# A landmark attention and two feed-forward layers in one kernel: the attention's pool released earlier, its last batch planned with more lead, two unit orders changed

## The chip, the cores and the metric

One core of a Trainium2 chip runs the whole program in one launch. The metric is the device time of that core in microseconds (us). The engines are TensorE (PE in the profile, its weight loads PEld), VectorE (DVE), ScalarE (ACT) and GpSimd (POOL); SyncE (SP) issues all DMAs of this kernel from one in-order queue. [...]

## The reference, cut to what matters

Shapes: `q`, `k`, `v` are 4 batches x 8 heads x 576 x 64; there are 2304 tokens of width 512; the first layer is 512 to 2048 to 512, the second 512 to 1536 (gate and value) to 512.

```python
A, Bm, C = sm(q, k_lm), sm(q_lm, k_lm), sm(q_lm, k)      # 32 landmarks: means over 18 rows
Z = Bm.T / (norm1(Bm) * norminf(Bm) + 1e-06)
for _ in range(6):
    Z = 2 * Z - Z @ Bm @ Z
x = A @ Z @ C @ v                                         # attention, then (B*S, H*D)
h = x @ w_in
x = np.maximum(0.01 * h, h) @ w_out                       # first layer
xn = x / np.sqrt(np.mean(x * x, -1, keepdims=True) + 1e-06) * rms_g
g, val = xn @ w_gate, xn @ w_val
out = (g * (1.0 / (1.0 + np.exp(-g))) * val) @ w_out2     # second layer
```

## The kernel before

Products are made in float32 precision out of three TensorE products of rounded parts: each operand is split into a `hi` and a `lo` (copy with rounding, then subtraction), and hi*hi, lo*hi, hi*lo are summed in PSUM. The splits keep VectorE, ScalarE and GpSimd busy beside TensorE.

Tokens go in blocks of 288: batch b is blocks j = 2b and 2b+1, eight in all. Three stages follow one another on TensorE.

**Attention and first layer.** For each batch and head group g, `chain` makes the Newton iteration and the small tile `wt` out of q, k and v; `form_m` multiplies `wt` with `w_in` into the weights `mm` of that batch (four column parts c, four buffers); `soft_a` makes the left softmax `at` of a block. The k buffers are two, so the k of batch 3 is loaded (`load_k`) when `soft_a` of block 5 has read those of batch 2. A unit (j, f) of the first layer is `ffn1_h` (L768) and `ffn1_y` (L834); there are 128, and the last ones are blocks 6 and 7. A finished block's sum goes to DRAM (L861), later `norm(j)` loads it (L982), squares it (L994 to L1000), lets TensorE sum over the features (L1005), and scales it (L1041); `load_x` (L1062) brings the two blocks of a batch back and `prep_x(b)` makes the seven split right-hand sides X of batch b (a Strassen-like scheme of seven products).

**Gate and value.** A unit (f, b) of the second layer, `gv`, has seven products of six matmuls (L1116), with seven additions and products after them on VectorE (`gv_rest`, L1171 to L1207), then a store of the result (L1198). `prep_w(f)` splits the weights W(f) into one of two homes, "even" and "odd", so W(f) can be made only when W(f-2) is through. The order of the 48 units is the list `seq`, written out by hand.

**Output.** `load_o` (L1256) loads the seven prepared tiles of `w_out2` (1536 KB each) into the homes that X and W leave: B11 and T2 where X(0) was, T3 and T1 where X(1) was, B21 and T4 where the last two W were, B22 where X(3) was. `load_u` (L1291) loads the results, `prep_u` splits them, and `out_pair` (L1359) makes nine pairs of 128-row blocks with seven products each.

Where things lie decides what can start: `att` is the pool of the attention; when it is released, `open_p2a` allocates the second layer's pool (`p2a`: loads of y, scratch, W "even", X(0)) in its place, and an instruction waits in hardware only for those old tiles that lie under its own. X(1) takes the space of the first half of `w_out` (free when no unit uses it any more), X(2) that of the second half (free after the last unit of the first layer), X(3) that of `mm` and `at`.

The order of every engine's instructions is fixed beforehand by a planner (`Order`). Each piece of work is a generator that yields an engine with an estimated duration and the conditions for it. The planner keeps its own clock and takes, among the pieces that can start soonest, the one with the smallest due time; a due time is a place in the list of units minus a lead from `PAR`. `pause(n)` is a wait of n ns that it assumes, for a DMA for instance. On the chip each engine then follows its list in order, and waits where the estimate was too short. `("cc", 1)` asks for one of the two buffers of a ring.

Of the kernel before, what the change touches and what calls it, by code (L numbers as in the profile page):

```python
# [8 lines left out]
F32 = mybir.dt.float32  # L9
F32R = mybir.dt.float32r  # L10
U32 = mybir.dt.uint32
# [7 lines left out]
P = 128  # L19
M = 32  # L20
# [5 lines left out]
PAR = {  # L26
    "bias": {"dve": 0, "act": 0, "pool": -300},
    "window": 100,
    "slope": 16.25,
    "t0": 25300,  # L30
    "unit": 2400,
    "chain": [18400, 20600, 27900, 42200],
    "soft": 5000,
    "form": 2600,
    "conv": 600,
# [4 lines left out]
    "h": 700,  # L40
    "y": -3900,
    "norm": 90000,
    "last": 60000,
    "second": 36800,
    "unit2": 5600,
    "pair": 14900,
# [133 lines left out]
def dvep(n):  # L180
    return [("dvep", int(n * 1.04) + 67)]
# [18 lines left out]
def pause(ns=0):  # L200
    return [(None, ns)]
# [3 lines left out]
def landmark_attention_then_two_ffns(  # L205
# [14 lines left out]
    B, NP, _, S = qT.shape  # L220
    NG = NP // 2
# [30 lines left out]
    def new(tag, pool, shape, dtype=F32):  # L252
        t = pool.tile(shape, dtype, tag=tag, bufs=rings[tag], name=tag)
        order.taken(tag, t)
        return t
# [38 lines left out]

    p1 = tc.alloc_tile_pool(name="p1", bufs=1, side="left", reuse_waits="tile")
    conv = tc.alloc_tile_pool(name="conv", bufs=1, side="right", reuse_waits="tile")
    att = tc.alloc_tile_pool(name="att", bufs=1, side="right", reuse_waits="tile")

    w_in_sb = [att.tile([P, NP, 512], U32, name=f"w_in{c}") for c in range(NC)]
    NFA = 8  # L300
    wo_hi, wo_lo = {}, {}
    home = {}
# [179 lines left out]
    def chain(b, g):  # L482
# [166 lines left out]
                order.free(pr)  # L649
        yield pe4(64), [(pa, 2), ("wt", 1), f"cv{b},{g}"]  # L650
        pw = bank(pa), bank(pa)
        wt = new("wt", att, [P, 2, M])
        for h, p, rows, lm in heads():
            nc.tensor.matmul(
                pw[p][rows, :M], t1[lm, :], z[lm, :], start=True, stop=True
# [219 lines left out]
    def open_p2a():  # L875
        pool = tc.alloc_tile_pool(name="p2a", bufs=1, side="right", reuse_waits="tile")
        p2["a"] = pool
        p2["ones"] = pool.tile([P, P], F32, name="ones")
        nc.gpsimd.memset(p2["ones"], 1.0)
        p2["power"] = pool.tile([P, 3], F32, name="power")  # L880
        nc.gpsimd.memset(p2["power"], -0.5)
        for i in range(2):
            home[i] = pool.tile([P, 4096], F32R, name=f"q{i}")
        home["even"] = pool.tile([P, 7 * KD * P], F32R, name="wt")
        home["y"] = pool.tile([P, 3, KD * SB], F32, name="yin")
        home["misc"] = pool.tile([P, 4 * 2 * SB + 2 * KD * P], F32, name="misc")
# [17 lines left out]
    def new_y():  # L904
        return spot("y_in", 0, (KD, SB))


    opened = {0: "p2a", 1: "p2a", 2: "w1_free", 3: "w1_free", 4: "w2_free", 5: "w2_free",
              6: "m_all", 7: "m_all"}

    def quarter(i, shape, dtype=F32R):
# [64 lines left out]
    def norm(j):  # L976

        if j < NB - 1:
            before = [f"normed{j - 1}"] if j else []
            yield sp(P * 16 * SB), ["p2a", f"y{y_of[j]}", ("y_in", 1)] + before  # L980
            y = new_y()
            nc.sync.dma_start(y, y_dram[y_of[j]])  # L982
            order.done(f"normed{j}")
            yield pause(3000), []
        else:
            yield pause(0), [f"y{y_of[j]}"]
            y = y_in[j]
        e = yield act(SB) + dvep(SB), [("tt", 2)]
        ss = [new_tt() for _ in range(2)]
        for d in range(KD):  # L990
            if d:
                e = yield act(SB) + dvep(SB), []
            if e == "act":
                nc.scalar.activation(ss[d // 2][:, d % 2, :], y[:, d, :], AF.Square)  # L994
            else:
                nc.vector.tensor_mul(ss[d // 2][:, d % 2, :], y[:, d, :], y[:, d, :])
        e = yield pool_dve(2 * SB), []
        engine[e].tensor_add(ss[0], ss[0], ss[1])
        e = yield pool_dve(SB), []
        engine[e].tensor_add(ss[0][:, 0, :], ss[0][:, 0, :], ss[0][:, 1, :])  # L1000

        yield pe4(40, 3), [("pa", 1)]
        pn = bank("pa")
        for t in range(3):
            nc.tensor.matmul(  # L1005
                pn[:T96, SB + t:SB + t + 1], ss[0][:, 0, t * T96:(t + 1) * T96],
                p2["ones"][:, :1], start=True, stop=True,
            )
        rr = p2["a"].tile([T96, 4, 3], F32, tag="rr", bufs=2, name="rr")
        yield dve(3), []  # L1010
        nc.vector.tensor_scalar(
            rr[:, 0, :], pn[:T96, SB:SB + 3], 1.0 / DM, EPS_RMS, op0=ALU.mult, op1=ALU.add
        )
        order.free(*ss)
        yield [("pool", 1000)], []
        nc.gpsimd.tensor_tensor(rr[:, 1, :], rr[:, 0, :], p2["power"][:T96, :], op=ALU.pow)

        yield dvep(3), []
        nc.vector.tensor_mul(rr[:, 2, :], rr[:, 1, :], rr[:, 1, :])
        yield dvep(3), []  # L1020
        nc.vector.scalar_tensor_tensor(
            rr[:, 3, :], rr[:, 2, :], -0.5, rr[:, 0, :], op0=ALU.mult, op1=ALU.mult
        )
        yield dvep(3), []
        nc.vector.scalar_tensor_tensor(
            rr[:, 2, :], rr[:, 3, :], 1.5, rr[:, 1, :], op0=ALU.add, op1=ALU.mult
        )
        yield dvep(SB), []
        dg = p2["a"].tile([T96, 3, T96], F32, tag="dg", bufs=1, name="dg")
        nc.vector.tensor_tensor(  # L1030
            dg, ident[:T96, :T96].unsqueeze(1).to_broadcast([T96, 3, T96]),
            rr[:, 2, :].unsqueeze(2).to_broadcast([T96, 3, T96]), op=ALU.mult,
        )
        yield pe4(SB), []
        nc.tensor.matmul(
            pn[:, :SB], p2["ones"][:T96, :], dg.rearrange("p t n -> p (t n)"),
            start=True, stop=True,
        )
        for d in range(KD):
            yield dve(SB), []  # L1040
            nc.vector.scalar_tensor_tensor(  # L1041
                y[:, d, :], y[:, d, :], g_sb[:, d:d + 1], pn[:, :SB],
                op0=ALU.mult, op1=ALU.mult,
            )
        order.free(pn)
        if j == NB - 1:
            order.done(f"x{j}")
            return
        yield sp(P * 16 * SB), []
        nc.sync.dma_start(y_dram[y_of[j]], y)  # L1050
        yield pause(2500), []
        order.free(y)
        order.done(f"xn{j}")

    def load_x(b):
        js = [j for j in (2 * b, 2 * b + 1) if j < NB - 1]
        yield sp(P * 16 * SB * len(js)), [f"xn{j}" for j in js] + [("y_in", len(js))] + (
            [opened[2 * b], opened[2 * b + 1]] if b < B - 2 else [f"normed{NB - 2}"]
        ) + ([f"y_in{b - 1}"] if b else [])
        for j in js:  # L1060
            y_in[j] = new_y()
            nc.sync.dma_start(y_in[j], y_dram[y_of[j]])  # L1062
        order.done(f"y_in{b}")
        yield pause(3000), []
        for j in js:
            order.done(f"x{j}")

# [36 lines left out]
        order.free(y0, *(y_sum[len(segs) - 1] if b == B - 1 else [y1]), ta, tb)  # L1104


    seq = [(f, b) for f, b in zip((0, 1, 0, 1, 0, 0, 1, 1), (0, 0, 1, 1, 2, 3, 2, 3))]
    seq += [(f, b) for f in range(2, NF2 - 2) for b in range(B)]
    seq += [(f, b) for bs in ((0, 1), (2,), (3,)) for f in (NF2 - 2, NF2 - 1) for b in bs]
    place = {k: i for i, k in enumerate(seq)}  # L1110

    def product(pp, f, b, i, k, first):
# [318 lines left out]
    with tc.manual_schedule():  # L1431
        def due(u):

            return PAR["t0"] + PAR["unit"] * u
# [75 lines left out]

        def start_second():
            yield pause(0), [f"a{NB - 1},{g}" for g in range(NG)] + [
                f"m{B - 1},{c},{g}" for c in range(NC) for g in range(NG)
            ]
            att.release()
            open_p2a()
            order.done("p2a")
            for j in range(NB):
                order.add(due2(j // 2), PAR["norm"], norm(j))
            for b in range(B):  # L1520
                order.add(due2(place[0, b]), PAR["prep"], load_x(b))
                order.add(due2(place[0, b]), PAR["prep"], prep_x(b))
            for f in range(NF2):
                order.add(due2(place[f, 0]), PAR["prep"], prep_w(f))
            order.add(due2(0), 0, gv(0))
            for i, k in enumerate(o_order):
                order.add(due_o(0) + i * PAR["pair"] // 7, 2 * PAR["prep"], load_o(k))
            for n in range(NG2):
                order.add(due_o(n), PAR["load_u"][min(n // 2, 1)], load_u(n))
                order.add(due_o(n), PAR["prep_u"], prep_u(n))  # L1530
            order.add(due_o(0), 0, out_pair(0))

        order.add(due(len(units)), PAR["second"], start_second())
        order.run()
        p2["a"].release()
        state["p1b"].release()
        p1.release()
        conv.release()


# [50 lines left out]
```

## Time and profile before

| | us |
|---|---|
| median of 3 runs (862.51 to 866.36) | 866.31 |
| the profiled execution's own time | 863.65 |
| its span, first to last instruction | 861.6 |
| TensorE busy | 825.5 |
| VectorE busy | 626.3 |
| ScalarE busy | 342.6 |
| GpSimd busy | 151.1 |

The first two stages end at about 438.8 and 715.9 us of the span. Busy is the union of an engine's instructions; matmuls are pipelined and their ends are modelled. In the timeline a row is the start, the length, the engine, the line, the operation, the tiles written and read, and how many instructions are merged; what stands in brackets is the idle time ahead of it and what ended it.

### The profile page before, as it was taken

The numbers are of one execution on the slowest core, as the hardware profiler recorded it, in microseconds if no ns is written. First come the engines' busy times: TensorE is split into PE (matmuls) and PEld (weight loads), VectorE is DVE, ScalarE is ACT, GpSimd is POOL, SyncE is SP. The second block draws the span as 40 slices with busy tenths as digits, with TensorE's granted clock in tenths as the row PEclk, the third lists the DMA queues.
The fourth block names the chain that finished last, engine by engine and source line by source line (L and its number), as shares of the span: only waits on it lengthen the run. The fifth ranks groups of instructions, "written<-read, shape, count | busy, mean of one in ns | idle before, by whom it ended". The sixth has DMA issues, their size and how long they took to land. (4 is left out here: it accounts for less than half of the span.)

```text
span 861.6 us, 17827 instructions
## 1 busy us (share of the span) xinstructions
PE 825.5 (96%) x6902; PEld 758.9 (88%) x6902; DVE 626.3 (73%) x1403; ACT 342.6 (40%) x814; POOL 151.1 (18%) x187
## 2 busy tenths in 40 slices
PE   4799999999999999999987999999999998999998
PEld 1488789988788786999887999999999998999998
DVE  6699784556565843768689877777777669799892
ACT  3676464445334633644534343333332223122120
POOL 2242241002120620122011312211222101000000
PEclk9599999999999999999989999999999999999999
DMA  9874774453723700566431223322221199663611
GB/s 326 319 250 144 244 238 144 165 186 101 221 89 110 238 30 1 181 203 229 141 110 56 91 104 106 105 104 105 105 102 45 64 349 380 189 183 98 180 42 49
DMA packets 80549, 131.97 MB, mean 153 GB/s; under 512 B 6224, under 2 KB 50256, under 8 KB 79568
## 3 DMA queue, kind: packets, MB, share of 16 engines
q1 hardware_dynamic: 80464, 130.84, 45.6%
q8 instruction: 54, 0.88, 0.4%
q14 instruction: 31, 0.25, 0.1%
HBM read 87.95 MB, written 42.86 MB: 152 GB/s over the span
## 5 line engine op out<-in xcount | busy, mean ns | idle before, releaser
L834 PE MATMUL py<-g_hi,w 128*128 128x288 f32 x1024 | 212.3, 300 | 0.0
L834 PEld LDWEIGHTS py<-g_hi,w 128*128 128x128 f32 x1024 | 165.0, 190 | 13.0 <-issue 12.1
L834 PE MATMUL py<-g_lo,w 128*128 128x288 f32 x512 | 151.6, 296 | 0.0
L768 PE MATMUL ph<-at,mm 128*128 128x288 f32 x768 | 127.4, 305 | 0.6 <-ACT hs L787 0.4
L768 PEld LDWEIGHTS ph<-at,mm 128*128 128x128 f32 x768 | 109.4, 191 | 15.5 <-ACT hs L787 4.8
L784 ACT ACTIVATE g_hi<-ph 128x288 fp32r<-128x288 f32 x128 | 52.5, 410 | 122.4 <-PE ph L768 107.7
L834 PEld LDWEIGHTS py<-g_lo,w 128*128 128x128 f32 x512 | 97.1, 190 | 0.0
L790 DVE TENSOR_TENSOR g_lo<-hs,g_hi 128x288 fp32r<-128x288 f32 x100 | 47.0, 470 | 57.0 <-ACT hs L787 54.6
L787 ACT ACTIVATE hs<-ph 128x288 f32<-128x288 f32 x128 | 52.1, 407 | 0.0
L1210 ACT ACTIVATE cc<-cc 128x288 f32<-128x288 f32 x48 | 21.4, 445 | 74.3 <-DVE cc L1207 74.3
L1116 PE MATMUL py<-w,wt 128*128 128x288 f32 x288 | 43.7, 302 | 4.2 <-DVE g_lo L1174 4.2
L1181 ACT ACTIVATE hs<-ph 128x288 f32<-128x288 f32 x48 | 19.7, 410 | 64.5 <-PE ph L1116 64.4
L1116 PEld LDWEIGHTS py<-w,wt 128*128 128x128 f32 x288 | 41.0, 194 | 4.5 <-DVE g_lo L1174 4.4
L1116 PE MATMUL py<-w,mm 128*128 128x288 f32 x288 | 42.6, 296 | 0.2 <-DVE g_lo L1174 0.2
L368 ACT ACTIVATE raw<-raw 128x512 f32<-128x512 f32 x52 | 35.3, 681 | 16.9 <-DMA raw<-w_val 10.1
L1184 DVE TENSOR_TENSOR cc<-g_hi,py 128x288 f32<-128x288 f32 x48 | 21.6, 450 | 26.7 <-PE py L1116 26.0
L1116 PEld LDWEIGHTS py<-w,mm 128*128 128x128 f32 x288 | 39.6, 188 | 0.7 <-DVE g_lo L1174 0.4
L790 POOL TENSOR_TENSOR g_lo<-hs,g_hi 128x288 fp32r<-128x288 f32 x28 | 23.8, 849 | 84.8 <-ACT hs L787 84.0
L735 PE MATMUL pa<-w_in,wt 64*32 64x512 f32 x256 | 33.7, 626 | 2.3 <-DVE x L689 1.3
L330 ACT COPY hs<-ph 128x288 f32<-128x288 f32 (+1 forms) x45 | 17.2, 382 | 43.6 <-PE ph L1359 36.6
L330 ACT CAST w<-misc 128x768 fp32r<-128x768 f32 (+1 forms) x23 | 17.6, 779 | 38.8 <-DVE misc L1329 20.7
L745 DVE TENSOR_TENSOR mm<-pa,mm 128x512 fp32r<-128x512 f32 x32 | 22.0, 689 | 15.2 <-ACT mm L330 15.0
(300 smaller groups left out, 1755.4 us busy)
## 6 DMA issues: line engine op xcount, KB each, us to landing
u_dram<-us SPq DMA_DIRECT2D x48, 288.0 KB, 2.1
wo_dram<-ct SPq DMA_DIRECT2D x42, 256.0 KB, 2.3
raw<-w_out SPq DMA_DIRECT2D x20, 512.0 KB, 4.4
y_dram<-ys SPq DMA_DIRECT2D x60, 144.0 KB, 2.5
yin<-y_dram SPq DMA_DIRECT2D x14, 576.0 KB, 4.4
yin<-u_dram SPq DMA_DIRECT2D x20, 384.0 KB, 6.2
raw<-w_gate SPq DMA_DIRECT2D x12, 512.0 KB, 4.0
raw<-w_val SPq DMA_DIRECT2D x12, 512.0 KB, 4.7
```

The source lines that it names most:

```text
L330: nc.scalar.copy(out, src)
L368: nc.scalar.activation(high.bitcast(F32), high.bitcast(F32), AF.Prelu, scale=2.0 ** -112, alpha=2.0 ** 32)
L735: nc.tensor.matmul(pm[lm, :], wt_in[b, g][rows, p], w_in_sb[c][rows, 2 * g + p, :].bitcast(F32), start=True, stop=True,)
L745: nc.vector.tensor_sub(lo, pm, hi.bitcast(F32))
L768: nc.tensor.matmul(ph[:, :SB], w[b, c][:, g, o:o + P], x[j][:, g, :], start=(n == 0), stop=(n == 3 * NG - 1),)
L784: nc.scalar.activation(g_hi[u], ph[:, :SB], AF.Prelu, alpha=0.01)
L787: nc.scalar.activation(hs, ph[:, :SB], AF.Prelu, alpha=0.01)
L790: engine[e].tensor_sub(g_lo[u], hs, g_hi[u].bitcast(F32))
L834: nc.tensor.matmul(yacc[i][d][:, :SB], w[f][:, d * P:(d + 1) * P], x[u], start=(f == f0 and n == 0), stop=(f == f1 - 1 and n == 2),)
L1116: nc.tensor.matmul(pp[:, :SB], w[f][:, i, c * P:(c + 1) * P], x[b][1][:, k, c, :], start=(first and n == 0), stop=(n == 5), skip_group_che ...
L1184: nc.vector.tensor_add(f32("c21", "cc"), t["u2"], pp["c"][:, :SB])
L1210: nc.scalar.activation(t["c12"], t["c12"], AF.Silu)
```

## The change

Six things are changed.

1. `w_in` and `wt` move out of `att` into a pool of their own, `wq`; the homes of X(0) are now made in `wq`, where `w_in` was (`free_w_in`), when the last `form_m` is through. `att` is released when the last `chain` and the last `soft_a` are through, and no longer waits for `form_m`.
2. The due time of the chain of batch 3 (with the loads of its k, q and v) lies 75000 ns ahead of its first unit and no longer 42200; `soft_a` and `form_m` of batch 3 lie 75000 ahead and no longer 60000.
3. The planner assumes 4200 ns and no longer 3000 for the loads of `norm` and `load_x`.
4. The scratch tile `dg` of `norm` is taken from the ring `cc` of the second layer.
5. `seq` begins (0,0) (1,0) (0,1) (1,1) (0,2) (1,2) (0,3) (1,3); the third pair was (0,2) (0,3), the fourth (1,2) (1,3).
6. `seq` ends (10,0) (11,0) (10,1) (11,1) and so on; it was (10,0) (10,1) (11,0) (11,1), then as now.

```diff
-    "chain": [18400, 20600, 27900, 42200],
+    "chain": [18400, 20600, 27900, 75000],
-    "last": 60000,
+    "last": 75000,
...
-    w_in_sb = [att.tile([P, NP, 512], U32, name=f"w_in{c}") for c in range(NC)]
+    w_in_sb = []
+    for i in range(2):
+        t = wq.tile([P, 4096], U32, tag=f"q{i}", name=f"w_in{i}")
+        t = t.rearrange("p (c a n) -> p c a n", a=NP, n=512)
+        w_in_sb += [t[:, 0], t[:, 1]]
...
-        wt = new("wt", att, [P, 2, M])
+        wt = new("wt", wq, [P, 2, M])
...
-        for i in range(2):
-            home[i] = pool.tile([P, 4096], F32R, name=f"q{i}")
...
-    opened = {0: "p2a", 1: "p2a", 2: "w1_free", 3: "w1_free", 4: "w2_free", 5: "w2_free",
+    opened = {0: "w_in_free", 1: "w_in_free", 2: "w1_free", 3: "w1_free", 4: "w2_free", 5: "w2_free",
...
-            yield pause(3000), []
+            yield pause(4200), []
...
-        yield dvep(SB), []
-        dg = p2["a"].tile([T96, 3, T96], F32, tag="dg", bufs=1, name="dg")
+        yield dvep(SB), [("cc", 1)]
+        cc = new("cc", p2["a"], [P, SB])
+        dg = cc[:T96, :].rearrange("p (t n) -> p t n", n=T96)
...
+        order.free(cc)
...
-        yield pause(3000), []
+        yield pause(4200), []
...
-    seq = [(f, b) for f, b in zip((0, 1, 0, 1, 0, 0, 1, 1), (0, 0, 1, 1, 2, 3, 2, 3))]
+    seq = [(f, b) for f, b in zip((0, 1, 0, 1, 0, 1, 0, 1), (0, 0, 1, 1, 2, 2, 3, 3))]
-    seq += [(f, b) for bs in ((0, 1), (2,), (3,)) for f in (NF2 - 2, NF2 - 1) for b in bs]
+    seq += [(f, b) for bs in ((0,), (1,), (2,), (3,)) for f in (NF2 - 2, NF2 - 1) for b in bs]
...
-                f"m{B - 1},{c},{g}" for c in range(NC) for g in range(NG)
+                f"chain{B - 1},{g}" for g in range(NG)
...
+        def free_w_in():
+            yield pause(0), [f"m{B - 1},{c},{g}" for c in range(NC) for g in range(NG)]
+            for i in range(2):
+                home[i] = wq.tile([P, 4096], F32R, tag=f"q{i}", name=f"q{i}")
+            order.done("w_in_free")
+
+        order.add(due(len(units)), PAR["second"], free_w_in())
```

## Rows read from the trace of the kernel before

**Rows 1.** The page, part 1: busy time, share of the span, instructions.

```profile
PE 825.5 (96%) x6902; PEld 758.9 (88%) x6902; DVE 626.3 (73%) x1403; ACT 342.6 (40%) x814; POOL 151.1 (18%) x187
```

**Rows 2.** Who waited for whom: total us, times, longest; TensorE's, then SyncE's at 410 to 440.

```profile
PE pa L1005 <- DVE misc L1000: 4.4, 2, 3.8
PE py L1116 <- DVE g_lo L1174: 4.4, 2, 4.2
...
PE py L1359 <- DMA mm<-wo_dram: 2.1, 1, 2.1
...
SPq L982 <- DMA y_dram<-ys: 5.6, 1, 5.6
```

**Rows 3.** Stretches: length, busy (instructions) of each engine, granted clock, DMA share, GB/s.

```profile
428.90:432.70 3.80, 0.01 (x1) 0.01 (x1) 2.96 (x6) 1.74 (x6) 0.00 (x0) 0.77 0.04 13
432.70:437.50 4.80, 4.78 (x22) 4.80 (x23) 3.30 (x8) 1.23 (x2) 1.31 (x1) 0.50 0.00 0
438.80:475.40 36.60, 31.63 (x222) 30.52 (x221) 34.72 (x76) 14.58 (x28) 5.51 (x6) 0.95 0.25 93
...
475.40:715.90 240.50, 240.50 (x1808) 239.99 (x1807) 178.79 (x377) 80.34 (x181) 48.87 (x52) 1.00 0.36 122
715.90:738.70 22.80, 18.16 (x136) 17.64 (x135) 20.01 (x32) 3.58 (x6) 0.00 (x0) 0.93 1.04 366
```

**Rows 4.** Timeline of SyncE's queue, 415 to 425, then ScalarE at 428.

```profile
415.88 0.92 SPq L1062 DMA_DIRECT2D yin<-y_dram  x2
416.90 1.73 SPq L861 DMA_DIRECT2D y_dram<-ys  x3
424.42 0.32 SPq L982 DMA_DIRECT2D yin<-y_dram  x1
...
428.34 0.45 ACT L994 ACTIVATE misc<-yin 128x288 f32<-128x288 f32 x1 [2.38 <-DMA yin<-y_dram]
```

**Rows 5.** Timeline: batch 3's keys and last chain product, last `form_m`, second `norm` load.

```profile
279.95 0.83 SPq L441 DMA_DIRECT2D kt<-kT  x2
...
334.89 0.32 PE L654 MATMUL pa<-rz,t 32*64 32x32 f32 x8
...
343.32 1.92 PE L735 MATMUL pa<-w_in,wt 64*32 64x512 f32 x16
...
347.62 0.42 SPq L982 DMA_DIRECT2D yin<-y_dram  x1
```

**Rows 6.** Timeline of VectorE while TensorE waits at 468 to 472.

```profile
469.56 1.42 DVE L929 TENSOR_TENSOR at<-misc,mm 128x576 fp32r<-128x576 f32 x2
470.90 0.44 DVE L1171 TENSOR_TENSOR g_hi<-hs,pa 128x288 f32<-128x288 f32 x1
...
471.93 0.44 DVE L1174 TENSOR_TENSOR g_lo<-g_hi,py 128x288 f32<-128x288 f32 x1
```

**Rows 7.** Timeline: `prep_w(2)` on ScalarE, GpSimd and VectorE.

```profile
479.92 0.61 ACT L330 CAST wt<-misc 128x512 fp32r<-128x512 f32 x1
...
485.32 0.73 POOL L965 TENSOR_TENSOR misc<-misc 128x256 f32<-128x256 f32 x1
...
485.44 1.16 DVE L929 TENSOR_TENSOR wt<-misc,wt 128x512 fp32r<-128x512 f32 x1 [0.32 <-ACT wt L330]
...
487.79 0.69 DVE L929 TENSOR_TENSOR wt<-misc,wt 128x512 fp32r<-128x512 f32 x1
```

**Rows 8.** Timeline: DMA issues at the end of gate and value, then TensorE's output stage.

```profile
687.51 0.32 SPq L1256 DMA_DIRECT2D q<-wo_dram  x1
...
719.59 0.43 SPq L1256 DMA_DIRECT2D mm<-wo_dram  x1
...
734.08 3.63 PE L1359 MATMUL py<-mm,at 128*128 128x256 f32 x18 [2.09 <-DMA mm<-wo_dram]
...
742.09 4.43 PE L1359 MATMUL py<-w,w 128*128 128x256 f32 x36
...
757.08 4.43 PE L1359 MATMUL py<-w,w 128*128 128x256 f32 x36
```

More of the change, by code (lines that the diff above doesn't have):

```diff
@@ L296, in landmark_attention_then_two_ffns @@
     conv = tc.alloc_tile_pool(name="conv", bufs=1, side="right", reuse_waits="tile")
+    wq = tc.alloc_tile_pool(name="wq", bufs=1, side="right", reuse_waits="tile")
     att = tc.alloc_tile_pool(name="att", bufs=1, side="right", reuse_waits="tile")
-    w_in_sb = [att.tile([P, NP, 512], U32, name=f"w_in{c}") for c in range(NC)]
+    w_in_sb = []
[3 more added lines that the diff above has]
+        w_in_sb += [t[:, 0], t[:, 1]]
     NFA = 8
@@ L1035, in norm @@
         nc.tensor.matmul(
-            pn[:, :SB], p2["ones"][:T96, :], dg.rearrange("p t n -> p (t n)"),
-            start=True, stop=True,
+            pn[:, :SB], p2["ones"][:T96, :], cc[:T96, :], start=True, stop=True,
         )
+        order.free(cc)
         for d in range(KD):
@@ L1537, in landmark_attention_then_two_ffns @@
         p1.release()
+        wq.release()
         conv.release()
```

## The prediction

> **What bounds the kernel now.** I read the page's busy times first: TensorE is busy 96% of the span, so whatever helps has to remove TensorE waits, and there are only 36 us of them, start-up and end included [rows 1]. The list of waits comes second: outside the start-up two of the three longest, 3.8 and 4.2 us, are waits for VectorE, in L1005 (the sum of a norm) and L1116 (gate and value); the third is a wait of the output stage for a DMA [rows 2]. The table of stretches shows what stands around them [rows 3], and that the middle of gate and value, 475.4 to 715.9, has no idle time at all: nothing is to be had there.
>
> Place A, end of the first layer. TensorE is idle from 428.9 to 432.7 and then runs until 437.5 at a granted clock of 0.50, the lower of its two levels [rows 3]. That is 3.8 us and half of 4.8: 6.2 us. The cause is `norm(6)`: its load was issued at 424.4, because SyncE had waited 5.6 us for the store of the same block [rows 2], and that store had shared the DMA engines with `load_x(1)`, issued at 415.9 between its pieces [rows 4]. The squares then waited another 2.4 us for the data, and TensorE, in order, stood behind L1005.
>
> Place B, first units of gate and value. A unit takes 240.5 / 43 = 5.59 us in the undisturbed middle; the five units from 438.8 to 475.4 took 36.6 instead of 28.0, so 8.6 us are lost [rows 3]. VectorE is busy 34.7 of those 36.6 us. In the 4.2 us wait it split X(3) for the next unit, while the addition that TensorE wanted, L1171, stood behind [rows 6]. VectorE is the bound here.
>
> Place C, first pair of the output. A pair takes 757.1 - 742.1 = 15.0 us [rows 8]. Going back two products of 2.14 from 742.1, the second pair began at 737.8, and the first took 21.9 us from 715.9: 6.9 us lost, 4.6 of them idle, the rest at a lower granted clock [rows 3]. The DMA engines are full in this stretch (share 1.04), and the last tile, B22, issued at 719.6, let TensorE go on at 734.1 [rows 8].
>
> Together 21.7 us lie in A, B and C. No row shows a fourth place as large that the change could reach.
>
> **The change part by part.** The sums are against the profiled execution's own 863.65 us; the median of the runs shown is 2.7 above it.
>
> *Earlier chain, pool given back earlier.* The chain of batch 3 starts with loads at 280 and ends at 335; the last `form_m` runs at 343, and the second norm's load comes at 347.6 [rows 5]. The load of the keys waits for buffers that `soft_a` of block 5 frees, and that due time is unchanged, so the chain can't start much before 280. With 33 us more lead it ranks ahead of the first layer's units and should end some 15 us sooner (estimate: the 55 us from load to end contain room for that, since its Newton steps alternate with units). `att` then goes back at about 320, not 345, and norms 0 to 5 and the split of X(0) move into the first layer by some 25 us. X(1) needs `w_out`'s first half, whose last use is 16 units of 18 matmuls before the stage's end; at 5.59 / 42 = 0.133 us a matmul [rows 3] that is 38 us before 438.8, about 400. Its loads come then, some 15 us before the 415.9 of now.
>
> What that is worth at A: the store of block 6 no longer shares the queue with `load_x(1)`, so the 5.6 us wait of SyncE shrinks to a normal landing, by 3 to 4 us, and VectorE doesn't split X(1) in the same microseconds. The longer assumed latency puts L1005 another 1.2 us back in TensorE's list. 3.8 us of idle time are covered by 3.5 + 1.2, and without the idle time I expect no stretch at 0.50. Between 0 and 6.2, I take 5.2.
>
> *First order.* X(3) is wanted by the seventh unit and not the sixth: 33.5 us after the stage's start, not 28.0. VectorE's bill up to there: an instruction on 288 columns takes the queue for 0.36 us and one on 576 for 0.67 (1.34 for two; 1.03 for one of each) [rows 6]. A unit has seven or eight of the small ones, some on other engines: 2.7 us. So five units cost 13.5, and of 36.6 busy us some 22 were other work (the end of norm 6, norm 7, X(2), X(3)). Before, the bill was 13.5 + 22 = 35.5 against 28.0: 7.5 short, near the 8.6 measured. After, norm 6 ends before the stage (2 us less): 6 x 2.7 + 20 = 36.2 against 33.5: 2.7 short. The difference is 4.8. Bounds: 0, if other work moves in, and 8.6.
>
> The price stands in `prep_w(2)`. W(2) goes where W(0) is, and W(0) is through one unit later, so one unit and not two covers its preparation. That took from 479.9 to 488.5, 8.6 us [rows 7]. W(0)'s last product ended near 475.4 + 5.6 = 481.0, so the first cast began 1.1 us ahead of that; the last part is wanted by the third product of the next unit but one, 5.6 + 1.6 = 7.2 us after it. 8.6 - 1.1 - 7.2 leaves 0.3 us late: nearly covered, by nothing to spare. [...] A piece of W(2) took 1.16 us on VectorE while GpSimd worked on another, and 0.69 alone [rows 7]. [...]
>
> *Last order.* X(0) is through one unit, 5.6 us, earlier, so the loads of B11 and T2 go out at about 682 and not 687.5 [rows 8], and those of the results likewise. From 687.5 to 734 the DMA engines work off one backlog (share 1.04 at its end). If it starts 5.6 us earlier, B22 lands at 728.4; the seventh product wants it at 715.9 + 6 x 2.14 = 728.7. T4 and B22 still can't leave before the last unit ends: two of 1536 KB at 366 GB/s are 8.6 us, which fits. The splits of the results start earlier too, and with them goes the wait for VectorE in this pair. Between 0 and 6.9, I take 5.3. W(11) is squeezed as W(2) is, with VectorE less loaded.
>
> *The rest.* `dg` in the ring `cc` holds one of two buffers for one product of norm 7; a unit's addition may wait for it, less than 1 us. `w_in` in its own pool costs no instruction. For this, the two W and possible waits of a chain that runs closer to its producers I take 1.3 (0 to 4.4, the total that any VectorE wait of a norm or unit shows now [rows 2]).
>
> Sum: 5.2 + 4.8 + 5.3 - 1.3 = 14.0. 863.65 - 14.0 = 849.7 for an execution like the profiled one, 852.3 if it shifts with the median; I take 851.
>
> **The rivals.**
> *The pool isn't given back earlier in fact.* For it: the chain hangs on key buffers [rows 5], and the hardware already waits tile by tile, so the planner's place means less than it seems. Then A keeps all but 1.2 us, B gains only by its order (6 x 2.7 + 22 - 33.5 = 4.7 short, 2.8 better), C stays 5.3, less 1.3: 8.0, or 857.
> *The tail is bound by bandwidth and by SyncE's order.* For it: the loads of T3 and T1 stand behind the results' loads, and T4 and B22 are issued when the last unit ends in either order. Then C gives 0 to 1: 9.2 in all, or 855.5.
> *The waits only move.* A planner that reorders everything may open as much as it closes: 861 to 868, about 864.
> *Slower: the squeezed W.* VectorE is still behind when W(2) is to be made, right after X(3). If a preparation takes 13.5 us and not 8.6, it is 5.2 late; TensorE idles that long and then runs at 0.50 as after A (2.4): 7.6 for each W. Two of them take 15.2 and the 14 are gone; this is the point from which it decides. At twice 8.6 it is 8.9 late, 11.3 each, 22.6 in all: about 873 less what remains, 872. Against it: VectorE has 25% free from 475 on [rows 3], and W(11) comes in such a stretch.
>
> **How the numbers follow.** Forecast 0.57 (its own range 845 to 857, from A 4 to 6, B 2.5 to 7, C 3 to 6.5); pool 0.16; tail 0.13; waits move 0.07; squeezed W 0.07. A measurement of this kernel can't tell less than 0.5%, 4.3 us, from no change. All of the forecast and nearly all of the next two lie beyond it: faster 0.84; the rest of these and most of the moved waits: same 0.09; slower 0.07. The range runs from 844 (nearly all of A, B and C) to 860 (the worse half of the two small-gain rivals); it leaves out the last two cases and the ends.
>
> **What would show it.** A: the load of norm 6 issued by about 421 and no idle time ahead of L1005; 0.50 gone there. B: X(3) split without a wait of 4 us, the first six units within some 37 us. W(2) ready within 0.5 us of its first use. C: first issue of L1256 a unit before X(0)'s present time, first pair within 17 us. The earlier chain: the last L654 near 320, norm loads from 320 on. Wrong would be a wait of L1116 for a piece of W, a first pair still near 22 us, or a last L654 still at 335.

## The result and the profile after

The changed kernel takes 854.21 us (median of 4 runs, 853.5 to 855.12), the kernel before 866.34 (4 runs, 862.51 to 866.55): a ratio of 0.9871 with a 95% interval of 0.9842 to 0.99. It is 12.1 us faster. The two profiled executions differ by less, 863.65 and 853.5 (spans 861.6 and 851.4), so the rows below share out 10.2 us.

Part 1 of the page of the changed kernel answers to [rows 1]. TensorE's busy time fell by 3.9 us and its idle time by the rest of the 10.2; VectorE's busy time is 4.9 us longer in a shorter span, but 3.9 of these are one instruction that was held (below) and did no more work.

```profile
PE 821.6 (96%) x6902; PEld 754.5 (89%) x6902; DVE 631.2 (74%) x1405; ACT 340.8 (40%) x816; POOL 147.2 (17%) x183
```

The list of TensorE's waits (total us, times, longest) answers to [rows 2]. Lines have moved: the sum of a norm is now L1008, the product that spreads a norm's scales L1039, gate and value L1120, the output L1363. The waits of 3.8 and 4.2 us and the one for a DMA are gone; a new one of 3.0 stands in L1039.

```profile
PE pa L1039 <- DVE cc L1034: 3.0, 1, 3.0
...
PE pa L1008 <- DVE misc L1003: 1.2, 1, 1.2
PE py L1120 <- DVE g_lo L1178: 1.2, 2, 1.0
```

The stretches (columns as in [rows 3]) are the end of the first layer, the wait, the first six units, the middle, the end of gate and value and the first output pair.

```profile
426.40:433.20 6.80, 6.80 (x54) 6.62 (x52) 4.24 (x6) 2.74 (x7) 2.89 (x3) 1.00 0.13 52
433.20:436.20 3.00, 0.05 (x1) 0.00 (x0) 2.90 (x5) 0.00 (x0) 2.08 (x2) 1.00 0.00 0
436.60:473.90 37.30, 35.78 (x262) 34.71 (x261) 34.50 (x73) 15.87 (x33) 8.78 (x7) 1.00 0.20 72
485.30:700.00 214.70, 214.70 (x1616) 214.35 (x1615) 157.46 (x336) 70.73 (x160) 41.70 (x47) 1.00 0.37 125
700.00:711.50 11.50, 10.08 (x68) 8.95 (x68) 11.30 (x22) 3.75 (x8) 0.00 (x0) 1.00 0.93 352
711.50:727.60 16.10, 15.32 (x129) 15.15 (x128) 16.10 (x26) 4.23 (x7) 0.00 (x0) 1.00 0.98 334
```

Place by place, in the profiled executions:

- A: gate and value begins at 436.6 and not 438.8, 2.2 us sooner. Norm 6's load goes out at 419.73 (424.42 before [rows 4]), since SyncE waits 1.6 us for the store and not 5.6 (its timeline, then its list of waits):

```profile
419.73 0.32 SPq L985 DMA_DIRECT2D yin<-y_dram  x1
...
SPq L985 <- DMA y_dram<-ys: 1.6, 1, 1.6
```

- B: the first six units take 37.3 us; before, the five units to 475.4 took 36.6 [rows 3] and the sixth 5.6, together 42.2. That is 4.9.
- The 40 units from the first one with W(2) take 226.2 us in place of 223.8: 2.4 lost, nearly all of it in the last two, where VectorE is busy almost without a gap (11.30 of 11.50 us) and TensorE idle for 1.4 us.
- C: the output stage takes 136.30 us in place of 142.09, 5.8 less. Nearly all of that is its first pair: 16.05 us (711.54 to 727.59) in place of 21.6, since in the kernel before the second pair begins at 737.50, 0.3 before the point that the prediction had worked out (TensorE's timeline, before):

```profile
737.50 1.88 PE L1359 MATMUL ph<-q,at 128*128 128x256 f32 x12
```

2.2 + 4.9 - 2.4 + 5.8 = 10.5, of a span that is 10.2 shorter; the two units between B and the 40 take 0.3 more.

What ended the new wait is in the timelines of GpSimd and VectorE, of the changed kernel, around norm 6 (start, duration, line).

```profile
430.31 0.85 POOL L1019 TENSOR_TENSOR rr<-rr,power 96x3 f32<-96x3 f32 x1 [21.93 <-DVE rr L1014]
431.13 1.43 POOL L1102 TENSOR_TENSOR misc<-yin 128x576 f32<-128x576 f32 x1
432.51 2.76 POOL L932 TENSOR_TENSOR w<-yin,w 128x576 fp32r<-128x576 f32 x2
...
431.19 4.10 DVE L1022 TENSOR_TENSOR rr<-rr 96x3 f32<-96x3 f32 x1 [1.03 <-POOL rr L1019]
```

L1022 multiplies 96x3 numbers. Its eight instructions have a median of 0.159 us; this one took 4.10, and ended when the third of three GpSimd instructions did (435.27). These are sums and splits of X(2), which the change has brought forward to this place: X(2)'s load goes out at 422.06 and not at 436.98 (SyncE's timelines).

The end of gate and value is read in VectorE's timeline and SyncE's.

```profile
687.88 0.46 DVE L1196 TENSOR_TENSOR us<-cc,g_lo 128x288 f32<-128x288 f32 x1 [0.57 <-ACT cc L1214]
...
699.32 0.46 DVE L1196 TENSOR_TENSOR us<-hs,cc 128x288 f32<-128x288 f32 x1 [1.68 <-DMA u_dram<-us]
...
700.06 0.95 DVE L1327 TENSOR_TENSOR misc<-yin 128x768 f32<-128x768 f32 x1
...
687.83 1.22 SPq L1202 DMA_DIRECT2D u_dram<-us  x1
689.09 1.79 SPq L1295 DMA_DIRECT2D q<-u_dram  x2
690.98 2.77 SPq L1295 DMA_DIRECT2D w<-u_dram  x2
693.85 1.69 SPq L1202 DMA_DIRECT2D u_dram<-us  x2
```

A unit's result is complete at 688.34, but SyncE, in order, first issues the loads of the operands' sources (L1295) and gets to its store at 693.85. The store lands 5.3 us later, at about 699.2. VectorE, in order too, waits 1.68 us for that buffer (0.9 for one in the kernel before), and from 700 on the splits of the output's operands (0.95 us each) queue up between the units' own additions.

### The profile page after: what moved, and what is told of

Same layout as the page of the kernel before. It is cut to its first block, busy times and chain, and to the rows that moved or that the text cites. A ratio compares the mean times of both kernels' runs of the same rounds, so it can differ in the third digit from the quotient of the medians.

```text
span 851.4 us, 17835 instructions
## 1 busy us (share of the span) xinstructions
PE 821.6 (96%) x6902; PEld 754.5 (89%) x6902; DVE 631.2 (74%) x1405; ACT 340.8 (40%) x816; POOL 147.2 (17%) x183
## 5 line engine op out<-in xcount | busy, mean ns | idle before, releaser
L839 PE MATMUL py<-g_hi,w 128*128 128x288 f32 x1024 | 210.7, 299 | 0.0
L773 PE MATMUL ph<-at,mm 128*128 128x288 f32 x768 | 127.5, 305 | 1.5 <-ACT hs L792 1.4
L773 PEld LDWEIGHTS ph<-at,mm 128*128 128x128 f32 x768 | 109.5, 191 | 16.7 <-ACT hs L792 6.0
L795 DVE TENSOR_TENSOR g_lo<-hs,g_hi 128x288 fp32r<-128x288 f32 x104 | 49.2, 473 | 55.3 <-ACT hs L792 54.8
L1120 PE MATMUL py<-w,wt 128*128 128x288 f32 x288 | 43.2, 298 | 0.0
L1120 PE MATMUL py<-w,mm 128*128 128x288 f32 x288 | 42.6, 296 | 0.3 <-DVE g_lo L1178 0.3
L373 ACT ACTIVATE raw<-raw 128x512 f32<-128x512 f32 x52 | 35.2, 680 | 16.5 <-DMA raw<-w_val 10.2
L1120 PEld LDWEIGHTS py<-w,wt 128*128 128x128 f32 x288 | 39.9, 189 | 0.5 <-DVE g_lo L1181 0.2
L1120 PEld LDWEIGHTS py<-w,mm 128*128 128x128 f32 x288 | 39.6, 188 | 0.8 <-DVE g_lo L1178 0.5
L1188 DVE TENSOR_TENSOR cc<-g_hi,py 128x288 f32<-128x288 f32 x48 | 21.6, 450 | 23.8 <-PE py L1120 23.8
L795 POOL TENSOR_TENSOR g_lo<-hs,g_hi 128x288 fp32r<-128x288 f32 x24 | 20.9, 872 | 66.7 <-ACT hs L792 64.5
L1196 DVE TENSOR_TENSOR us<-cc,g_lo 128x288 f32<-128x288 f32 x46 | 22.9, 498 | 12.2 <-ACT cc L1214 12.2
L1196 DVE TENSOR_TENSOR us<-hs,cc 128x288 f32<-128x288 f32 x45 | 26.9, 599 | 5.6 <-DMA u_dram<-us 1.7
```

The lines of the kernel that those rows point to most:

```text
L373: nc.scalar.activation(high.bitcast(F32), high.bitcast(F32), AF.Prelu, scale=2.0 ** -112, alpha=2.0 ** 32)
L773: nc.tensor.matmul(ph[:, :SB], w[b, c][:, g, o:o + P], x[j][:, g, :], start=(n == 0), stop=(n == 3 * NG - 1),)
L795: engine[e].tensor_sub(g_lo[u], hs, g_hi[u].bitcast(F32))
L839: nc.tensor.matmul(yacc[i][d][:, :SB], w[f][:, d * P:(d + 1) * P], x[u], start=(f == f0 and n == 0), stop=(f == f1 - 1 and n == 2),)
L1120: nc.tensor.matmul(pp[:, :SB], w[f][:, i, c * P:(c + 1) * P], x[b][1][:, k, c, :], start=(first and n == 0), stop=(n == 5), skip_group_che ...
L1188: nc.vector.tensor_add(f32("c21", "cc"), t["u2"], pp["c"][:, :SB])
```

## The experiments

Medians and ratios are against runs of the kernel before on the same chip. "From the keys" is the time from batch 3's load of the keys, since the time of that load moves between executions (279.95 us in the kernel before, 280.34 in the changed kernel, 281.32 with the condition undone). The runs come from three chips, on which the medians of the kernel before are 864.77, 865.8 and 866.55. The changed kernel was not run again on these chips, so a difference between an edit and the changed kernel of less than some 2 us is not settled by medians.

**The orders, one at a time.** The kernel before, with the first order alone:

```diff
-    seq = [(f, b) for f, b in zip((0, 1, 0, 1, 0, 0, 1, 1), (0, 0, 1, 1, 2, 3, 2, 3))]
+    seq = [(f, b) for f, b in zip((0, 1, 0, 1, 0, 1, 0, 1), (0, 0, 1, 1, 2, 2, 3, 3))]
```

> The kernel before with the first order of units alone: the third and fourth pair become (0,2) (1,2) (0,3) (1,3). The bill theory (VectorE's work up to the unit that wants X(3) is the bound; the end of norm 6 still lies in this stretch) gives 6 x 2.7 + 22 = 38.2 us of work against 33.5, 4.7 short where it was 7.5: a gain of 2.8 us, a ratio near 0.997, and the first six units in about 39.5 us. The theory that the order alone made the 4.9 us found at this place gives 4.9 us, 0.994, six units in 37.3 us. The theory that it only helps once the norms are moved ahead gives 0 to 1 us. All three expect the wait ahead of the first unit and the output stage to stay as before.

861.66 us (7 runs), ratio 0.995 (0.9928 to 0.9973). Gate and value takes 273.41 us where it took 277.16: 3.75 gained. Its first six units take 37.8 us (42.2 before): 4.4 gained, so the theory of the order alone (37.3) comes nearer than the bill (39.5). The wait of L1005 at norm 6 stays:

```profile
PE pa L1005 <- DVE misc L1000: 4.3, 2, 3.7
```

The last order alone:

```diff
-    seq += [(f, b) for bs in ((0, 1), (2,), (3,)) for f in (NF2 - 2, NF2 - 1) for b in bs]
+    seq += [(f, b) for bs in ((0,), (1,), (2,), (3,)) for f in (NF2 - 2, NF2 - 1) for b in bs]
```

> The kernel before with the last order of units alone: (10,0) (11,0) (10,1) (11,1). The theory that the output's first pair gains 5.8 us and the splits of its operands then collide with the last units' additions on VectorE, 2.5 us back, gives 3.3 us, a ratio near 0.996, with the last eight units in some 47 us and not 44.7. The rival that the 2.5 us come from elsewhere in the change gives 5.8 us, 0.993, and undisturbed last units. The rival that the tail is bound by bandwidth gives under 1 us.

862.78 us (10 runs), ratio 0.9961 (0.9946 to 0.9976). The output stage is 6.3 us shorter (135.80 after 142.09), gate and value 2.9 longer (280.05). So the loss at the end of gate and value comes with the last order, and VectorE's list of waits shows the same store:

```profile
DVE us L1192 <- DMA u_dram<-us: 1.7, 1, 1.7
```

**Both orders undone in the changed kernel**, which leaves the pool, the lead and the latency:

> The changed kernel with both orders of units put back; the pool, the lead, the longer latencies and the shared scratch stay. The places theory: 2.2 us ahead of the first unit as in the changed kernel, and about 2.0 us in the first units because the end of norm 6 lies ahead of them (13.5 + 20 against 28.0, 5.5 short where it was 7.5): 4.2 us, a ratio near 0.995. The theory that the order made all of the gain in the first units gives 2.2 us, 0.9975. The output's first pair takes 21.9 us again in both.

857.28 us (4 runs), ratio 0.9917 (0.9892 to 0.9941). This is 7 us of gain, more than either theory gave. Gate and value begins 156.2 us from the keys (156.3 in the changed kernel, 158.8 before) and takes 274.17, 3.0 less than before: giving the pool back earlier empties the first units too, not only place A. Without the last order the waits of the first output pair are back (2.1 us for a split, 1.7 and 0.7 for a DMA). The parts don't add: in the first six units the first order alone is worth 4.4, the pool alone 3.2, both together 4.9. (In this execution the first unit ran in part at a lower clock, 0.64 from 436 to 439 us, the last section's subject, and took 7.3 us after 5.8 in the changed kernel; so the pool alone may be worth more.)

**The lead undone** ("chain" back to 42200, "last" to 60000):

> The changed kernel with the due times of batch 3's attention put back (42200 and 60000). If the release of the pool no longer waits for the last form_m, that alone moves the norms ahead: the last chain product comes near 335 instead of 329 and the time is that of the changed kernel within 1 us (ratio to before 0.987 to 0.989). If the lead is what makes the gain ahead of and in the first units, some 4 us of it are lost: 0.992.

854.77 us (4 runs), ratio 0.9882 (0.9859 to 0.9905), not to be told from the changed kernel. The last chain product runs at 335.29, where the kernel before had it, against 329.28 with the lead (both in TensorE's timeline, lead undone first):

```profile
335.29 0.32 PE L659 MATMUL pa<-rz,t 32*64 32x32 f32 x8
```
```profile
329.28 0.32 PE L659 MATMUL pa<-rz,t 32*64 32x32 f32 x8
```

It also gives a second reading of the stall. Here two GpSimd instructions run beside norm 6 and not three, and L1022 takes 2.76 us, again until the last of them ends (434.69):

```profile
431.89 1.43 POOL L1086 TENSOR_TENSOR misc<-yin 128x576 f32<-128x576 f32 x1
433.28 1.41 POOL L1102 TENSOR_TENSOR misc<-yin 128x576 f32<-128x576 f32 x1
...
431.95 2.76 DVE L1022 TENSOR_TENSOR rr<-rr 96x3 f32<-96x3 f32 x1 [0.97 <-POOL rr L1019]
```

**The condition undone.** The pool waits for batch 3's last `form_m` again:

```diff
-                f"chain{B - 1},{g}" for g in range(NG)
+                f"m{B - 1},{c},{g}" for c in range(NC) for g in range(NG)
```

> Only the condition for giving back attention's pool goes back to that of before (batch 3's last form_m instead of its last chain product); the new lead, both orders and the latency stay. Theory: the earlier release is what brought norm 6's load forward, and the run without the new lead has shown that the lead alone is worth at most 1 us. Then A is lost: gate and value begin 158 to 160 us after the load of the keys (156.3 in the changed kernel, 158.8 before), the load of X(0) is back near 390 or later, and 857 to 858 is measured. Rival: the lead does as much by itself, since the first condition is met a little later anyway: 854 to 855, with gate and value at 156 to 156.5.

856.84 us (6 runs), ratio 0.9893 (0.9871 to 0.9915). The time is near the theory's, but not the place that it named. X(1)'s load goes out at 419.18, once more right before norm 6's (422.39); in the changed kernel it went at 399.07. Norm 6 now comes after the first products of gate and value, which begin at 151.5 us from the keys, 5 sooner than in the changed kernel, with waits of 0.7 and 0.5 there. What is late instead is X(2), loaded at 446.87, in the first six units, which grow by 8.7:

```profile
PE pa L1120 <- ACT w L335: 2.8, 1, 2.8
```

From the keys to the ninth unit's first addition the four kernels need 214.3 (before), 210.7 (condition undone), 207.3 (lead undone) and 206.8 us (changed). The condition is worth 3.9 of the 7.4 in the profiled executions, 2.6 by the medians and 1.9 by the ratios, whose intervals overlap; the lead 0.4. Two parts of the change no run undoes by themselves, the move of `w_in` into a pool of its own and `dg` in the ring; what they are worth alone is not known.

**The latency undone** (4200 back to 3000):

> Only the assumed latency of a load goes back from 4200 to 3000. Theory of the forecast: the longer latency keeps the squares of the last norms out of TensorE's and VectorE's lists until the data are there and is worth about 1.2 us at the end of the first layer: 855.4, with a wait for a load in front of the sums of the norms again. Rival: the wait that is left there (3.0 us in L1039) has nothing to do with the load, so the latency is worth nothing: 854 to 854.5, the wait of L1039 still 2 to 3 us.

854.68 us (4 runs), ratio 0.9875 (0.9854 to 0.9895), with the same 3.0 us in L1039 and 1.2 in L1008. The rival holds: the longer latency is worth nothing that these runs can tell.

**X(2) kept off GpSimd.** Its sums and splits go to VectorE; GpSimd keeps the norm's own step:

```diff
-            e = yield pool_dve(n), []
+            e = yield (dvep(n) if b == 2 else pool_dve(n)), []
...
-            e = yield pool(n) + dvep(n), []
+            e = yield (dvep(n) if no_pool else pool(n) + dvep(n)), []
```

> The sums and splits of X(2) are kept off GpSimd (VectorE does them); the norm's own step stays there. Theory: VectorE's step of 96x3 in norm 6 took 4.10 us because three GpSimd instructions of X(2) ran beside it, and that was the wait of 3.0 us in L1039. Then the step takes 0.2 us, the wait is below 0.5, gate and value begin 3 us earlier (153.3 us after the load of the keys, where it was 156.3), and 851.2 is measured if VectorE has room, 852 to 853 if the 8 us of GpSimd's work moved to it come due among the first six units (37.3 us there become 38 to 39). Rival: the step is held by something else (its inputs, the order of VectorE's list): it stays at 3 us or more, the wait too, and the time is 854 to 856.

850.86 us (5 runs), ratio 0.9836 (0.9813 to 0.986). VectorE's timeline has L1022 at the same microsecond, and short:

```profile
431.19 0.16 DVE L1022 TENSOR_TENSOR rr<-rr 96x3 f32<-96x3 f32 x1 [1.03 <-POOL rr L1019]
```

The wait of L1039 is gone, gate and value begins at 433.37, 153.9 us from the keys, and the first six units take 38.3 us in place of 37.3, since VectorE has more to do: 2.4 gained, 1.0 given back. That GpSimd's instructions cause the loss that remained at A is shown. Between the medians lie 3.3 us, more than these two executions place; the rest stays open (half clock, in the last section, may take part of it in some executions).

**The operands' preparation planned later** ("prep_u" 6000 to 0, and to 3000):

> The output operands are planned 6 us later (lead of 0 in place of 6000). Theory: the 2.5 us lost in the last two units of gate and value are the operands' sums and splits of 0.95 us that stand between the units' own additions on VectorE; moved behind them, gate and value takes 272.5 us in place of 274.9, and the first pair of the output keeps its 16 us since its operands' loads don't move: 852. Rival: the work is only pushed into the first pair, which waits for it on VectorE: gate and value 272.5, the output stage 138 to 139 in place of 136.3, the time 854 to 855.

> As the run with a lead of 0, with half of the lead kept (3000). Theory: gate and value 273.5 us, the output stage 136.3 as in the changed kernel: 853. Rival: the work is shared out between the two places and the sum of both stages stays at 411.2 us: 854.

853.75 us (4 runs), ratio 0.9867 (0.9847 to 0.9887), and 854.07 us (4 runs), ratio 0.9869 (0.985 to 0.9887). Both theories fall: gate and value takes 276.5 and 276.8 us, not less than before the edit (274.9). What it takes more lies in its first unit (7.2 and 7.3 us for 5.8, at a granted clock of 0.50 from 436 to 439 us and of 0.57 from 439 to 442); the last two units of the two runs take 13.8 and 14.3 us, and 13.8 in the changed kernel. The splits come 0.8 and 2.2 us later, no more than gate and value's own end does (0.9 and 2.2). So the lead doesn't set their place; and VectorE's wait for the store (1.7 and 2.1 us) is still ahead of them. That moved the suspicion from the splits to the store.

**The last eight units' stores issued by ScalarE**, so that they don't stand behind SyncE's loads:

```diff
-            yield sp(P * 8 * SB), [f"half{i}"]
-            nc.sync.dma_start(
+            if i < 40:
+                yield sp(P * 8 * SB), [f"half{i}"]
+            else:
+                yield act(30), [f"half{i}"]
+            (nc.sync if i < 40 else nc.scalar).dma_start(
```

> The stores of the last eight units of gate and value are issued by ScalarE and not by SyncE; nothing else is changed. Theory: the 1.5 to 2.5 us lost in the last units come from one store of 288 KB that stands behind the loads of the first results and lands after 5.3 us in place of 2.1; VectorE, in order, waits 1.7 us for its buffer and has no room left for the splits. From another queue the store lands sooner, the wait of 1.7 us goes, and the two units take 11.2 to 11.8 us in place of 12.9: 852 to 853. Rival 1: the DMA engines are full, so a store takes as long from any queue; the wait stays and 854 is measured. Rival 2: the splits alone fill VectorE there; the wait goes, but the two units still take 12.5 or more.

852.18 us (5 runs), ratio 0.9847 (0.9822 to 0.9872). A result complete at 691.72 (VectorE) is stored at 691.75 (ScalarE's queue):

```profile
691.26 0.46 DVE L1196 TENSOR_TENSOR us<-cc,g_lo 128x288 f32<-128x288 f32 x1 [0.57 <-ACT cc L1217]
...
691.75 0.33 ACTq L1205 DMA_DIRECT2D u_dram<-us  x1
```

VectorE's wait for a store is gone, and two units take 11.9 us in place of 12.9 (by VectorE's first addition of each; in the changed kernel from 688.38 to 701.29). The reason that the expectation gave is half wrong: a store lands no sooner after its issue (median 6.4 us in the stretch from 686 to 705, 5.0 in the changed kernel); it is issued 5.5 us sooner after its data are complete. The splits alone keep 0.7 of the loss. Two us lie between the medians, but the runs of the two kernels overlap (850.67 to 854.75 here), so the units' own 1.0 is the safer figure.

**Both edits together:**

> Both edits: X(2) kept off GpSimd, and the last eight units' stores issued by ScalarE. Theory: the two are far apart in time (430 and 700 us) and add: 3.0 from the first (851.1 was its median against 854.2) and 1 to 2 from the second: 849 to 850. Rival: the second is worth nothing, 851.

848.93 us (5 runs, 848.42 to 849.7), ratio 0.9805 (0.9783 to 0.9827). This version beats both kernels, by 17 and 5 us. The same two units are at 5.95 and 5.96 us, so what the splits cost, 0.7, stays.

## Why the prediction was right, and where its sum was off

The forecast, 851 with 844 to 860, was for 3 us less than the 854.2 measured. By the terms it had 849.7 for an execution like the profiled one, and 853.5 was measured, 3.8 more. The terms, against the profiled executions:

- **A, 5.2 forecast, 2.2 measured: mis-sized.** The mechanism at norm 6's sum was right: norm 6's load goes out at 419.73 (by about 421 was forecast, 424.42 before [rows 4]), SyncE waits 1.6 us and not 5.6 for the store, and no idle time stands ahead of its sum (the 1.2 us of L1008 are norm 7's, in the first units). Before, this place lost 6.2; the new wait gives 3.0 back, and two waits for ScalarE (L773, at 396.5 and 416.6), which the kernel before did not have there, another 1.0. The step that failed is "3.8 us of idle time are covered": it asked whether norm 6's data would be there and not what VectorE's three small steps behind it would meet. The work brought forward with the pool included GpSimd's, which fell on the first of these steps and held it for 4.10 us. Without it the wait is gone. In this one place the rival by which waits only move came half true.
- **The longer latency, 1.2 within A: nothing that can be told.** The run without it has the same time within the noise, and the same wait at norm 6.
- **The earlier chain: its size was off, and it doesn't carry the gain.** The last chain product came at 329.28 and not near 320, the second norm's load at 330.93 (347.62 before [rows 5]), 17 us sooner and not 25. A lead that is worth 6 us to the chain is worth 0.4 to the kernel; the condition, which no longer waits for `form_m`, is worth 1.9 to 3.9. So one sign of being wrong that the prediction named, a last L654 still at 335, was no sign: with the lead undone that product comes at 335.29, and the time is the same.
- **B, 4.8 forecast, 4.9 measured.** Six units in 37.3 us, "within some 37". VectorE is busy for 34.5 of them, and the run that gives it GpSimd's part of X(2) needs 1.0 more, so it is the bound there, as the prediction said. But its bill gave 2.8 to the order and 2.0 to norm 6's earlier end, and each alone measures more (4.4 and 3.2). They cover in part the same loss, and that the sum came out within 0.1 is in part luck. The bill also took 36.6 us as VectorE's busy time where [rows 3] show 34.7; with 34.7 both of its sides fall alike, and the difference stays 4.8.
- **The squeezed W(2): right.** Its last part is through VectorE at 485.43, TensorE runs on past 485.32, where the first unit with it begins, and no wait of L1120 for a piece of W is in the list. The rival that would have made the kernel slower had no footing.
- **C, 5.3 forecast, 5.8 measured.** First pair 16.05 us; the waits for a DMA are gone, and the run with the last order alone has the same gain in this stage (6.3). (Before, the first pair took 21.6 us and not 21.9, so 6.6 was to be had and not 6.9.) The rival of a tail bound by bandwidth falls, with the DMA share at 0.98 in that stretch.
- **The rest, 1.3 forecast, 2.4 measured: right sign, wrong place.** It was set for `cc` and the W; the list shows neither. A term for the two W no run shows: in the changed kernel no GpSimd instruction runs beside the preparation of W(2) (476 to 487 us), and its pieces on 512 columns take 0.68 to 0.69 us on VectorE. What cost was the last order's own shadow: the loads that it brought forward delay a store, and the splits that it brought forward fill VectorE in the last units. The prediction followed these loads to their use in the output stage and not to what stands behind them on SyncE.

The rival that the pool isn't given back earlier in fact gave 857, and undoing the condition measured 856.84. That agreement is luck: the rival had most of A lost and the first units better by 2.8, and that run has gate and value begin 5 us sooner and its first six units 8.7 us longer than the changed kernel. (The tail rival's 855.5 is 855.8 by its own terms.)

## What to carry to other kernels

When work is moved forward, price it where it lands as well as where it leaves: here two of three terms held, and what was missing was moved work that met a short chain of tiny instructions (3.0 us) and an in-order queue (about 1). Before a load is issued earlier, list the stores that will stand behind it on that queue, and how many buffers are left while they wait. And two knobs that were changed along with the one that mattered, a lead and a latency, were worth nothing that can be told from the noise; one run with each undone shows that.

## What the runs showed of the hardware that was not expected

A VectorE instruction on 96x3 numbers (L1022) was held at norm 6 for as long as GpSimd had instructions running one behind the other: 4.10 us beside three, 2.76 beside two, 0.16 beside none, at the same place of the program. That it is held on where one GpSimd instruction follows another is not general. In the run with the condition undone the same line, a little later in the program (norm 7), met two GpSimd instructions and was held for the first alone: it ended at 448.69, with the first (448.67), while the second ran until 449.37 (GpSimd, then VectorE).

```profile
447.79 0.88 POOL L961 TENSOR_TENSOR misc<-misc 128x256 f32<-128x256 f32 x1
448.63 0.74 POOL L966 TENSOR_TENSOR misc<-misc 128x256 f32<-128x256 f32 x1
...
448.00 0.69 DVE L1022 TENSOR_TENSOR rr<-rr 96x3 f32<-96x3 f32 x1
```

What decides between the two no run here shows. The prediction had seen one VectorE instruction slowed beside GpSimd, a piece of W at 1.16 us and not 0.69, 0.47 more [rows 7], and not one held through several instructions.

The wait of 3.0 us is followed by half clock in some executions and not in others. (The granted clock of TensorE is recorded as 1.00 or 0.50, and as nothing else, in the traces of the kernel before and of the changed kernel; half clock is the 0.50, and a figure between is the mean of a stretch.) Of the six profiled executions that have it, two (the changed kernel and the one with the latency undone) stay at 1.00; the other four fall to 0.50, 0.57, 0.64 and 0.50 in one of the two stretches of three microseconds that begin at 436, though TensorE has the same instructions in the same order up to there as in the changed kernel. The deepest is the run with the stores on ScalarE, in the stretch from 436 to 442 (granted clock 0.54):

```profile
436.00:442.00 6.00, 4.91 (x18) 4.62 (x19) 3.86 (x11) 2.10 (x4) 0.14 (x1) 0.54 0.01 3
```

The first six units of that execution take 39.7 us, 2.4 more than in the changed kernel. That is more than half of the 4.1 us between it (854.75) and the fastest of the same kernel (850.67), whose mean granted clock is 0.986 and not 0.982; that the low clock is what separates the two is likely and not shown, since the fastest left no profile. The two profiled kernels without the wait stay at 1.00 from 428 to 448. What decides between the two outcomes after the same wait no run here shows.
